# Output projections ahead of SSM steps for the free PSUM bank, and a re-set of the planner's rules

## The chip, the cores and the metric

The kernel runs on one core of a Trainium2 chip. The metric is the device time in microseconds; the time before is the median of three runs, 708.05 us (708.03 to 708.15). One more execution was taken with the hardware profiler; the numbers of the profile come from it.

The core has five engines that run side by side and meet at semaphores: TensorE (PE; its weight loads are shown apart as PEld), VectorE (DVE), ScalarE (ACT), GpSimd (POOL) and SyncE (SP), which here issues DMAs.

## The reference

Two independent branches share one launch, and their outputs stand side by side in a [1, 2048, 1280] bf16 result.

- **Branch A, a diagonal state-space model (SSM).** x is [2048, 640]. Per state, `Lam_bar = exp(dt * Lam)` with complex `Lam`; the input matrix is scaled by `(Lam_bar - 1) / Lam`; the recurrence is `h[t] = Lam_bar * h[t-1] + B_bar x[t]`, and `y[t] = 2 Re(C h[t]) + D * x[t]`.
- **Branch B, attention with 32 query heads of width 20 and one shared key and value head.** `q = x wq`, `k = x wk`, `v = x wv`; `softmax(q k^T / sqrt(20)) v` for every head without a mask; then the heads, 640 wide, times `wo`.

## The kernel before

**Order.** The kernel is written out by a planner that runs on the host while the program is built. `Schedule` simulates the engines with a duration for each step (`Op`); whenever an engine is free, `pick` chooses among the ready steps the one with the lowest `prio`. On TensorE a step in another tiling mode gets 1.2 added to a priority above 1, and a step that would run more than `slack["pe"]` ns into a due urgent step is held back. `Emitter` then writes each engine's stream in that order, with semaphores where data demand them. So the constants of the planner set only the order, and which engine takes a tile; the work itself is fixed. `planned` made 32 plans, each with due times jittered by up to `SPREAD` tiles, replayed each with random DMA delays, and kept the best by its own estimate.

**Attention.** The scores are 2048 tiles of 128 keys x 512 query columns (4 query blocks x 8 groups of 4 heads x 16 key chunks x 4 heads). `attention` goes through them in steps. A step uses one of two sets of three PSUM banks (`CHUNKS = (3, 3)`, tiles `SC`): TensorE writes up to three score tiles as matmuls on 32 rows of the array each (`score`, mode S). ScalarE then takes the exponential of two or three of them at once into `PR` (`fill`, line 1489). VectorE can take the third bank instead ("own" tile): it makes a bf16 pattern from the score with an integer add and max into a buffer of `BIG` (`fill_d`, line 863), and three shifted copies of it, most of them made two at a time by GpSimd as 64-bit integer adds (`copy`, line 1804) and the rest by VectorE. The four copies are multiplied with four scaled versions of V (`VS`), so a VectorE tile needs four V matmuls and a ScalarE tile one (`VP`). V matmuls run four at once on 32 columns each (`pv`, mode C) into the bank `MB` kept for them.

**Which tiles go to VectorE.** `want_own` and `want_d` allow one if the count stays under `SHARE` = 0.29 of (tiles so far - 16), not in the last 20 tiles, if copy buffers are free and if `behind()` is false; `in_time` asks that VectorE can read the third bank at most `SPARE` ns after ScalarE ends with the other two; `WAITING` bounds the third-bank tiles not yet read. `behind()` is true when the next SSM unit's last step has not started `LAG` tiles after its due tile and an SSM step marked late could be run.

**The other work.** Everything else takes turns on one free PSUM bank (`MISC = 1`), handed out by `manager`: of the tasks whose due tile has come and which are ready, the one with the lowest class, and among these the one due first. Class 1 are query projections (`q_task`); class 2 are the SSM tasks: ten products `C B` (`cb_task`), 20 units of five state blocks in four time blocks (`unit_task`, followed on VectorE by rotations, two scans and `W`), and 20 output steps (`y_task`). The output projections `o_task` of the query blocks, five each, were class 2 as well. A task's product steps run as groups of four matmuls, or ride one piece at a time on a score step's free rows (`ride`, `board`), as long as more than `KEEP_C` steps are left. Copies from PSUM go to `stg` and from there to the output. The last query block's output projections, and three partial sums of them made ahead, end the kernel. Filler matmuls on zeros (`VZ`) keep TensorE active where it would fall idle.

**Queues.** SP issues nearly all DMAs in the planned order; GpSimd's stream has only the library load, constants and the copies.

Of the kernel before, what the change touches and what calls it, by code (L numbers as in the profile page):

```python
# [24 lines left out]
class Op:  # L25
# [5 lines left out]
    def __init__(self, eng, fns, dur, deps=(), prio=5, reads=(), writes=(), prev=None, gate=None, hook=None,  # L31
                 dma_key=None, land=0.0, tail=0.0, mode="F", load=0.0, port=False):
        self.eng, self.fns, self.dur = eng, list(fns), dur
        self.deps, self.prio, self.prev = list(deps), prio, prev
        self.reads, self.writes = list(reads), list(writes)
        self.gate, self.hook = gate, hook
        self.dma_key, self.land, self.tail = dma_key, land, tail
        self.mode, self.load, self.late = mode, load, False
        self.port, self.after, self.due, self.table, self.twice, self.fence, self.lands = port, [], None, None, None, None, None
        self.psum = any(k[0] == "B" and k[1:].isdigit() for k in self.reads)  # L40
        self.start = self.end = None
        self.clear = 1e18
        self.seq = self.idx = 0


class Schedule:
# [13 lines left out]
    EARLIER = {"dve": 40.0, "act": 8.0}  # L60
# [4 lines left out]
    def __init__(self, seed=0):  # L65
        self.rng = random.Random(seed) if seed else None
        self.t = 0.0
        self.pending = {e: [] for e in self.ENGINES}
        self.free = {e: 0.0 for e in self.ENGINES}
        self.order = []  # L70
        self.events = []
        self.procs = []
        self.dma_free = {}
        self.n = 0
        self.mode = None
        self.late_from = 0.0
        self.loads = []
        self.sources = {e: [] for e in self.ENGINES}
        self.slack = {"pe": 60.0, "dve": 150.0}
        self.port_free = {"dve": 0.0, "pool": 0.0}  # L80
        self.port_last = {"dve": None, "pool": None}
        self.port_wanted = False
        self.pipe, self.table = 0.0, None
# [374 lines left out]
NQB, NKC, NGG = 4, 16, 8  # L458
NTILE = NQB * NGG * NKC * 4
# [6 lines left out]
class Build:  # L466
# [73 lines left out]
        shares.update({f"OPT{k}": [f"BA{i}_{c}" for i in range(2) for c in range(NC)] for k in self.EARLY_O})  # L540
        return shares

    SPREAD = 12.0
    PLANS, REPLAYS = 32, 12

    def planned(self):

        best = None
        gc.disable()
        for seed in range(self.PLANS):  # L550
            plan = copy.copy(self)
            plan.s = Schedule(seed)
            plan.program()
            try:
                plan.s.run()
            except RuntimeError:
                continue
            cold = self.COLD * self.quiet(plan.s.order)
            if best is not None and max(op.end for op in plan.s.order) + cold > best[0] + self.MARGIN:
                continue  # L560
            em = Emitter(self.nc, plan.s.order, [b.key for b in plan.banks], self.shared())
            em.plan()
            end = sum(em.replay(random.Random(k)) for k in range(self.REPLAYS)) / self.REPLAYS + cold
            if best is None or end < best[0]:
                best = (end, em)
        gc.enable()
        return best[1]
# [160 lines left out]
    def quads(self):  # L728
        return self.QUADS and self.started

    GRAIN, KEEP_C = 256, 5

    def ride(self, bank, steps):

# [697 lines left out]
    def fill_now(self, op, i, n):  # L1432
# [6 lines left out]
        if s.t >= op.due or not self.can_d() or len(self.d_free()) < len(self.SHIFTS):  # L1439
            return True  # L1440
        if len(self.d_banks()) >= self.WANT:
            return True
# [5 lines left out]
                    return False  # L1448
        return True

    WANT = 1

    def fill(self, op, i):
        p = self
        t, banks = self.slots[i]
        n = min(self.cap[i], NTILE - self.tile_n)
        extra, used, own = [], set(), None
        if n == 3 and self.want_own() and self.in_time(i):
            own = self.take_d(used)
        if own is not None:  # L1460
            n = 2
        while len(extra) < 4 - self.cap[i] and self.want_d(len(extra), own is not None):
            m = self.take_d(used)
            if m is None:
                break
            extra.append(m)
        tiles = [self.take_tile(used) for _ in range(n)]
        h = self.pr_take(n)
        keys = [f"PR{h.index + x}" for x in range(n)]
        ents = []  # L1470
        for x, m in enumerate(tiles):
            b, kc, j = self.score(op, m, t[:, 512 * x:512 * x + 512], banks[x])
            ents.append((b, kc, j, p.PR[:, h.index + x, :]))
        first = [] if own is None else [self.fill_d(op, own, banks[2])]
        if first:
            other = self.slot_last[1 - i][0]
            begin = self.s.t + self.mmt(512, 4) + 200
            if other.eng == "act":
                begin = max(begin, other.start + other.dur if other.start is not None else self.s.t + other.dur)
            first[0].due = begin + 2 * (0.8333 * 1024 + 64) - self.REFILL  # L1480
        for m in extra:
            self.fill_d(op, m)
        n_mm = len(op.fns)
        self.board(op, used)
        op.reads = sorted(set(op.reads))
        op.dur = self.mmt(512, n_mm + (len(op.fns) > n_mm))
        op.load = 128.0 * n_mm
        dst = p.PR[:, h.index:h.index + n, :]
        ex = self.act(lambda e: e.activation(dst, t[:, 0:512 * n], ACT.Exp, scale=1.0 / UNIT),  # L1489
                      0.8333 * 512 * n + 64, table="exp",  # L1490
                      deps=[op], reads=[b.key for b in banks[:n]], writes=keys, prio=0.5,
                      gate=lambda: all(x.taken and x.left == 0 and self.s.done(x.users) for x in h.prev))

        def on_start(_):
            h.taken, h.left, h.prev = True, n, []
            self.waiting.remove(h)
        self.waiting.append(h)
        ex.hook = on_start
        self.slot_last[i] = [ex] + first
        for (b, kc, j, rhs), key in zip(ents, keys):  # L1500
            self.pvq[b][j].append((p.VP[:, kc, 0:32], kc, rhs, key, ex, h, "VP"))
            self.pv_filled[b] += 1
# [29 lines left out]
        return any(x is not None and x.taken and x.left for x in self.owner[at:at + 3]) \  # L1532
            or any(x.left for h in self.waiting for x in h.prev)

    WAITING = 2
    REFILL = 900.0

    def want_own(self):
        if self.tile_n >= NTILE - self.LAST or self.d_count + 1 > self.SHARE * (self.tile_n - 16) or self.behind():
            return False  # L1540
        if sum(1 for o in self.firsts if o.start is None) >= self.WAITING:
            return False
# [3 lines left out]
    def in_time(self, i):  # L1546
# [7 lines left out]
        for o in self.firsts:  # L1554
            if o.start is None:
                at = max(at, s.seen(o.deps[0], "dve")) + 605
        return at + 605 + 110 <= begin + 2 * 512 * 0.8333 + 64 + self.SPARE

    SPARE = 100
    firsts = []  # L1560
    LAG = 120

    def behind(self):

        while self.next_unit < NQB * NC:
            w = self.w_op.get(divmod(self.next_unit, NC))
            if w is None or w.start is None:
                return self.tile_n > self.unit_due[divmod(self.next_unit, NC)] + self.LAG \
                    and any(o.late and self.s.ready(o) is not None for o in self.s.pending["dve"])
            self.next_unit += 1  # L1570
        return False

# [32 lines left out]
        self.tile_n += 1  # L1605
        return 64 * b + 4 * self.rem[b][j].popleft() + j

    EARLIER, LATER = 4, 5
    AHEAD, CAP, ROOM = 10, 2, 4

    def d_block(self):

# [52 lines left out]
            op.reads = sorted(set(op.reads))  # L1665
        return Op("pe", [], self.mmt(512), prio=self.ALONE, mode="S", load=128.0, hook=hook)

    ALONE, TASK, PV = 1.9, 0.95, 2.0
    EV, P1, COPY, COPY1 = 0.52, 0.5, 0.56, 0.6
    P1OWN = 0.42  # L1670
    CLOSE, PVEV = 0.3, 0.3

# [87 lines left out]

    BACKLOG = 9
    LAST = 20
    POOL_LAST = 10

    def pool_source(self):

        s = self.s
        can = [d for d in self.d_open if d[1].end is not None and s.seen(d[1], "pool") <= s.t]
        if not can or len(self.d_free()) < 2 or self.tile_n > NTILE - self.POOL_LAST or self.adds_op.start is None:
            return None  # L1770
# [499 lines left out]
        self.cb_done = True  # L2270

    C_DUE = 200
    CB_FROM, CB_STEP = 300, 20

    def cb_of(self, cd, lo, hi):
        return self.xbT[:, cd, lo:hi]
# [146 lines left out]
        return lambda: all(o.start is not None for o in ops)  # L2423


    Q_FROM, Q_STEP = (0, 30, 110, 190), 15
    SSM_FROM, SSM_TO, Y_STEP, GRACE = 150, 1780, 20, 40
    unit_due = {}

    def background(self):  # L2430
        T = self.tasks
# [9 lines left out]
                T.append((64 * (b + 1), 0, lambda b=b: self.den_ready(b), lambda bank, b=b: self.den_task(b, bank)))  # L2441
        for qb in range(NQB):
            for k in range(5):
                T.append((512 * (qb + 1) + 30 + 40 * k if qb < NQB - 1 else NTILE - 8, 2, lambda qb=qb: self.o_ready(qb),
                          lambda bank, qb=qb, k=k: self.o_task(qb, (4, 0, 1, 2, 3)[k], bank)))
        for k in self.EARLY_O:
            T.append((NTILE - 72, 2, lambda: self.parts_ready(), lambda bank, k=k: self.o_task(NQB - 1, k, bank, True)))
# [8 lines left out]
        for i, (unit, tb, c, ri) in enumerate(jobs):  # L2456
# [5 lines left out]
            n = i - len(jobs) + NC  # L2462
# [4 lines left out]
        if rng is not None:  # L2467
            T[:] = [(t[0] + (rng.uniform(-self.SPREAD, self.SPREAD) if 0 < t[0] < self.SSM_TO else 0.0),) + t[1:] for t in T]
        T.sort(key=lambda t: t[0])
# [115 lines left out]
```

## Time and profile before

| | |
|---|---|
| Median of 3 runs | 708.05 us |
| Profiled execution, first to last instruction | 707.2 us |
| ScalarE / TensorE busy | 691.6 us / 692.6 us |
| VectorE / GpSimd busy | 618.2 us / 466.5 us |
| Score tiles by ScalarE / VectorE | 1479 / 569 |
| First and last exponential start | 18.7 us, 698.2 us |

Busy time counts overlapping instructions once. Consecutive exponentials overlap in the profile, and the ends of matmuls are modelled, so neither share says by itself that an engine can do no more: the distance from one start to the next does. A row of a group gives engine, operation, output and inputs, shape, count, then busy us, mean ns of one, and the idle time of that engine just before, with what ended it. A row of a stage gives the stretch in us, its length, and for each engine the busy time with the number of instructions.

### The profile page before, as it was taken

Reading aid. Unit: us, or ns where it says so; the run is one execution under the profiler, and the core shown is the slowest. Engines: PE = TensorE matmul, PEld = TensorE weight load, DVE = VectorE, ACT = ScalarE, POOL = GpSimd, SP = SyncE. Lnnn points to the kernel's source line nnn. Section 1 sums busy time; section 2 is a strip of 40 time slices with the busy share of each in tenths; the row PEclk is TensorE's granted clock in tenths of the full one; section 3 lists DMA queues with packets and bytes.
Section 4 is the critical chain, followed back from the end, with each engine's and each line's share of the span. In section 5 each row is a group of like instructions: output and inputs, shape, how many; then the busy total and the mean of one; then the engine's idle time right before and its main releaser. Section 6 shows DMA issues by size and latency. Waiting matters only on the chain.

```text
span 707.2 us, 26749 instructions
## 1 busy us (share of the span) xinstructions
PE 692.6 (98%) x11246; PEld 248.8 (35%) x11248; DVE 618.2 (87%) x1181; ACT 691.6 (98%) x705; POOL 466.5 (66%) x794
## 2 busy tenths in 40 slices
PE   9999999999999999999999999999999999999997
PEld 5322233443233433333433332324333333343323
DVE  7899899999988878868779998999999999977794
ACT  7999999999999999999999999999999999999996
POOL 4266682037877667745967777787777768678881
PEclk9999999999999999999999999999999999999999
DMA  9677551020120001101401010120000001110001
GB/s 224 160 162 174 124 136 53 27 45 9 32 66 12 9 19 28 52 8 34 62 20 29 18 27 25 44 56 18 16 14 20 13 23 27 39 27 19 24 15 39
DMA packets 77589, 34.44 MB, mean 49 GB/s; under 512 B 58350, under 2 KB 77470, under 8 KB 77470
## 3 DMA queue, kind: packets, MB, share of 16 engines
q1 hardware_dynamic: 76506, 32.44, 19.2%
q8 instruction: 90, 1.47, 0.9%
q10 hardware_dynamic: 964, 0.29, 0.2%
q14 instruction: 29, 0.24, 0.1%
HBM read 11.53 MB, written 9.75 MB: 30 GB/s over the span
## 4 chain that ended last, share of the span: by engine, by line
ACT 56%; PE 42%; issue 0%; DVE 0%
ACT PR L1489 56%; PE MB L726 17%; PE MB L796 10%; PE SC L726 10%; PE MB L806 4%; PE SC L1154 1%; PE SC L722 0%; PE MB L1271 0%; DVE mab L1160 0%; DVE BIG L863 0%; PE SC L1210 0%; ACT PR L2051 0%; DVE pvsb L858 0%; DVE M L862 0%; DVE PR L964 0%
## 5 line engine op out<-in xcount | busy, mean ns | idle before, releaser
L1489 ACT ACTIVATE PR<-SC 128x1024 bf16<-128x1024 f32 (+1 forms) x681 | 676.7, 1199 | 5.0 <-PE SC L726 4.2
L1804 POOL INT64_ADD BIG<-BIG x759 | 454.2, 615 | 214.8 <-DVE BIG L863 75.0
L863 DVE TENSOR_SCALAR BIG<-SC 128x512 int16<-128x512 f32 x534 | 360.7, 686 | 61.2 <-PE SC L726 53.1
L726 PE MATMUL SC<-QT,KT 32*128 32x512 bf16 x2013 | 266.4, 384 | 6.6 <-ACT PR L1489 3.3
L726 PE MATMUL MB<-BIG,VS 128*32 128x512 bf16 x2276 | 254.6, 384 | 0.4 <-DVE pvsb L1871 0.3
L726 PE MATMUL MB<-PR,VP 128*32 128x512 bf16 x1479 | 205.0, 385 | 0.0
L726 PEld LDWEIGHTS SC<-QT,KT 32*128 32x128 bf16 x2013 | 68.0, 90 | 179.2 <-ACT PR L1489 117.5
L726 PEld LDWEIGHTS MB<-BIG,VS 128*32 128x32 bf16 x2276 | 59.3, 94 | 63.5 <-issue 42.1
L726 PEld LDWEIGHTS MB<-PR,VP 128*32 128x32 bf16 x1479 | 48.9, 94 | 49.7 <-issue 38.5
L796 PE MATMUL MB<-CT,W 128*32 128x320 bf16 (+2 forms) x1000 | 53.6, 301 | 0.1
L863 DVE TENSOR_SCALAR BIG<-BIG 128x1024 int16<-128x1024 int16 (+1 forms) x100 | 39.8, 424 | 2.6 <-PE MB L726 2.3
L796 PE MATMUL MB<-CA,W 128*32 128x512 bf16 (+1 forms) x640 | 36.4, 302 | 0.6 <-issue 0.5
L796 PE MATMUL MB<-xaT,BA 128*32 128x256 bf16 x800 | 31.8, 275 | 0.2 <-DVE BIG L1311 0.2
L806 PE MATMUL MB<-xaT,BT 32*128 32x256 bf16 x160 | 30.9, 272 | 0.7 <-ACT PR L1489 0.7
L806 PE MATMUL MB<-diagD,xaT 32*128 32x128 bf16 x320 | 31.3, 217 | 0.0
L796 PEld LDWEIGHTS MB<-CT,W 128*32 128x32 bf16 x1000 | 23.0, 96 | 15.0 <-issue 6.8
L806 PEld LDWEIGHTS MB<-diagD,xaT 32*128 32x128 bf16 x320 | 17.7, 92 | 29.4 <-ACT PR L1489 20.4
L796 PE MATMUL MB<-xaT,BT 128*32 128x256 bf16 x640 | 26.7, 274 | 0.0
L2056 DVE CAST stg<-MB 128x512 bf16<-128x512 f32 x35 | 23.9, 683 | 1.8 <-PE MB L796 1.4
L858 DVE TENSOR_TENSOR prod<-MB,tab 128x1024 bf16<-128x1024 f32 x20 | 24.3, 1217 | 0.9 <-PE SC L726 0.6
L863 DVE TENSOR_SCALAR BIG<-MB 128x512 int16<-128x512 f32 x35 | 23.8, 680 | 0.1
L796 PE MATMUL MB<-WO,OP 128*32 128x128 bf16 (+1 forms) x480 | 23.4, 301 | 0.0
(169 smaller groups left out, 473.8 us busy)
## 6 DMA issues: line engine op xcount, KB each, us to landing
out_dram<-stg SPq DMA_DIRECT2D x31, 128.0 KB, 1.8
qd<-BIG SPq DMA_DIRECT2D x20, 128.0 KB, 2.2
QT<-qd SPq DMA_DIRECT2D x28, 80.0 KB
OP<-pvsb SPq DMA_DIRECT2D x105, 20.0 KB
rdP<-recs SPq DMA_DIRECT2D x105, 20.0 KB
lbd<-BA SPq DMA_DIRECT2D x5, 320.0 KB, 3.0
CT<-in_B_x_dram SPq DMA_DIRECT2D x2, 640.0 KB, 5.3
BA<-in_A_B_re_dram SPq DMA_DIRECT2D x1, 800.0 KB, 7.9
```

Source lines behind the costliest of these rows:

```text
L726: return lambda e: e.matmul(out, lhsT=lhsT, rhs=rhs, start=start, stop=stop, **kw)
L796: x = e.matmul(out[32 * j:32 * j + 32], lhsT=lhsT[:, 32 * j:32 * j + 32], rhs=rhs, start=start, stop=r.end is tag, tile_position=(0, 32 * ...
L806: return lambda e: e.matmul(out, lhsT=lhsT[at], rhs=rhs[at], start=False, stop=r.end is tag, tile_position=(32 * row, 0), skip_group_check ...
L858: return lambda e: e.tensor_tensor(out, a, b, op)
L863: return lambda e: e.tensor_scalar(out, a, s1, s2, op0=op0, op1=op1)
L1154: prev = self.pe([lambda e, x=x, c=c, n=n, at=at: e.matmul(bank.cols(n * x, n * x + n), lhsT=p.wks[:, 128 * c:128 * c + 128], rhs=p.xbT[:, ...
L1489: ex = self.act(lambda e: e.activation(dst, t[:, 0:512 * n], ACT.Exp, scale=1.0 / UNIT), 0.8333 * 512 * n + 64, table="exp", deps=[op], re ...
L1804: op.fns.append(lambda e: e.int64_add(words(dst), words(src), add))
L2056: ev = self.dve(lambda e: e.tensor_copy(st, bank.ap), 645, deps=[prev], reads=[bank.key], writes=[key], prio=self.EV, gate=(lambda: last.e ...
```

## The change

The order's rules are set anew; no step is added or removed.

- Output projections of the first three query blocks go from class 2 to class 1, due at 512 (qb + 1) + 31.4 + 40 k.
- `behind()`: `LAG` 120 to 190.4 tiles, and a late SSM step counts only if it can start within `SOON` = 2731 ns.
- Admission of VectorE tiles: `WAITING` 2 to 3, `SPARE` 100 to 148, `REFILL`, `AHEAD`, `LATER`. The cap `SHARE` stays. `MISC_FIRST` is new and off.
- TensorE's `slack` 60 to 192.8 ns; `KEEP_C` 5 to 3; priorities `ALONE`, `PV`, `COPY1`; `POOL_LAST` 10 to 6; due times `CB_FROM`, `CB_STEP`, `Q_STEP`, `Y_STEP`, `GRACE`.
- One plan, with seed 69701 and a jitter of 14.5 tiles, in place of the best of 32 with 12.

```diff
-        self.slack = {"pe": 60.0, "dve": 150.0}
+        self.slack = {"pe": 192.807, "dve": 150.0}
...
-    SPREAD = 12.0
-    PLANS, REPLAYS = 32, 12
+    SPREAD = 14.468
+    SEEDS, REPLAYS = (69701,), 12
...
-        for seed in range(self.PLANS):
+        for seed in self.SEEDS:
...
-    GRAIN, KEEP_C = 256, 5
+    GRAIN, KEEP_C = 256, 3
...
-        if n == 3 and self.want_own() and self.in_time(i):
+        if n == 3 and not (self.MISC_FIRST and self.want_d() and self.can_d()) and self.want_own() and self.in_time(i):
...
-    WAITING = 2
-    REFILL = 900.0
+    WAITING = 3
+    REFILL = 905.623
...
-    SPARE = 100
+    SPARE = 148.045
     firsts = []
-    LAG = 120
+    LAG, SOON = 190.385, 2730.774
...
-                    and any(o.late and self.s.ready(o) is not None for o in self.s.pending["dve"])
+                    and any(o.late and (self.s.ready(o) or 1e18) <= self.s.t + self.SOON for o in self.s.pending["dve"])
...
-    EARLIER, LATER = 4, 5
-    AHEAD, CAP, ROOM = 10, 2, 4
+    EARLIER, LATER = 4, 6
+    AHEAD, CAP, ROOM = 14, 2, 4
...
-    ALONE, TASK, PV = 1.9, 0.95, 2.0
-    EV, P1, COPY, COPY1 = 0.52, 0.5, 0.56, 0.6
+    ALONE, TASK, PV = 1.686, 0.95, 1.9
+    EV, P1, COPY, COPY1 = 0.52, 0.5, 0.56, 0.83
...
-    POOL_LAST = 10
+    POOL_LAST = 6
...
-    CB_FROM, CB_STEP = 300, 20
+    CB_FROM, CB_STEP = 358.689, 15.665
...
-    Q_FROM, Q_STEP = (0, 30, 110, 190), 15
-    SSM_FROM, SSM_TO, Y_STEP, GRACE = 150, 1780, 20, 40
+    Q_FROM, Q_STEP = (0, 30, 110, 190), 12.835
+    O_FROM, O_STEP, O_CLASS = 31.404, 40, 1
+    SSM_FROM, SSM_TO, Y_STEP, GRACE = 150, 1780, 16.662, 48.136
...
-                T.append((512 * (qb + 1) + 30 + 40 * k if qb < NQB - 1 else NTILE - 8, 2, lambda qb=qb: self.o_ready(qb),
+                T.append((512 * (qb + 1) + self.O_FROM + self.O_STEP * k if qb < NQB - 1 else NTILE - 8, self.O_CLASS if qb < NQB - 1 else 2, lambda qb=qb: self.o_ready(qb),
```

More of the change, by code (lines that the diff above doesn't have):

```diff
@@ L1449, in fill_now @@
         return True
-    WANT = 1
+    WANT, MISC_FIRST = 1, False
     def fill(self, op, i):
```

## The prediction

> **What bounds the kernel now.** I read the page first, for the shares and for the chain that ended last.
>
> ```profile
> span 707.2 us, 26749 instructions
> PE 692.6 (98%) x11246; PEld 248.8 (35%) x11248; DVE 618.2 (87%) x1181; ACT 691.6 (98%) x705; POOL 466.5 (66%) x794
> ACT 56%; PE 42%; issue 0%; DVE 0%
> ```
>
> Two engines look full, so the second view is the groups of instructions with the shapes kept apart. It says how the 2048 score tiles are shared.
>
> ```profile
> L1489 ACT ACTIVATE PR<-SC 128x1024 bf16<-128x1024 f32 x562 | 528.2, 1115 | 4.4 <-PE SC L726 4.2
> L1489 ACT ACTIVATE PR<-SC 128x1536 bf16<-128x1536 f32 x118 | 168.8, 1603 | 0.6 <-PE MB L726 0.5
> L863 DVE TENSOR_SCALAR BIG<-SC 128x512 int16<-128x512 f32 x534 | 360.7, 686 | 61.2 <-PE SC L726 53.1
> L863 DVE TENSOR_SCALAR BIG<-MB 128x512 int16<-128x512 f32 x35 | 23.8, 680 | 0.1
> L726 PE MATMUL MB<-BIG,VS 128*32 128x512 bf16 x2276 | 254.6, 384 | 0.4 <-DVE pvsb L1871 0.3
> L726 PE MATMUL MB<-PR,VP 128*32 128x512 bf16 x1479 | 205.0, 385 | 0.0
> ```
>
> VectorE turned 534 + 35 = 569 tiles into probabilities (2276 = 4 x 569 confirms it: such a tile is multiplied with V four times), ScalarE 1479, in exponentials two or three tiles wide. Third comes what one exponential costs from start to start, since they overlap and the mean of one is longer than its turn. Two stretches hold one width only (windows 112 to 130.1 and 156 to 163.4), and the view of the exponential's line has the first and last start.
>
> ```profile
> L1489 ACT ACTIVATE PR<-SC 128x1536 bf16<-128x1536 f32 x15 | 20.5, 1742 | 0.0
> L1489 ACT ACTIVATE PR<-SC 128x1024 bf16<-128x1024 f32 x9 | 8.4, 1131 | 0.0
> L1489 ACT ACTIVATE PR<-SC x681: 787/1127/1830, 18.7 to 698.2; 128x1024 bf16<-128x1024 f32 x142, 128x1536 bf16<-128x1536 f32 x28, 128x512 bf16<-128x512 f32 x1
> ```
>
> A turn is (20.5 - 1.74) / 14 = 1.340 us for three tiles and (8.4 - 1.13) / 8 = 0.909 us for two, so a tile taken off ScalarE is worth 0.431 us. From the first start to the last are 679.5 us, of which 562 x 0.909 + 118 x 1.340 = 669.0 are turns and about 10.5 us are gaps. Head 18.7 us, stream 679.5, tail 9.0: that is the span. The median of the runs, 708.05, is 0.85 us above it. So the time is the number of ScalarE tiles, plus gaps, plus head and tail. The chain of waits says who sets the pace.
>
> ```profile
> ACT PR L1489 <- PE SC L726: 4.2, 6, 1.4
> PEld SC L726 <- ACT PR L1489: 117.5, 286, 0.7
> PEld SC L726 <- DVE BIG L863: 36.6, 86, 0.6
> PEld MB L726 <- issue: 84.3, 371, 0.4
> ```
>
> The score matmuls were released by ScalarE 286 times, the exponentials by TensorE visibly 6 times. ScalarE leads; TensorE follows closely.
>
> **The change part by part.** No work is removed. The planner keeps its cap of 0.29 x (tiles so far - 16) VectorE tiles and stops them 20 tiles before the end, so at most 0.29 x 2012 = 583 are allowed; 569 were taken. Where the rest was lost is in the busy time of VectorE on the score banks by stage (columns: stretch, its length, busy time and, in brackets, instructions, nearly all of them such tiles; then granted clock, DMA share, GB/s):
>
> ```profile
> 20.00:110.00 90.00, 43.28 (x66) 1.00 0.61 142
> 110.00:160.00 50.00, 7.07 (x12) 1.00 0.15 38
> 160.00:210.00 50.00, 29.98 (x44) 1.00 0.14 32
> 210.00:410.00 200.00, 106.39 (x157) 1.00 0.13 27
> 410.00:610.00 200.00, 127.92 (x191) 1.00 0.11 27
> 610.00:700.00 90.00, 51.73 (x77) 1.00 0.08 20
> ```
>
> *Withholding (behind: LAG 120 to 190, SOON).* Between 110 and 160 us 12 tiles were taken where the next 50 us took 44. There the rule withholds them: the first SSM unit is due at tile 150, so from tile 270 on: at three tiles and 679.5 / 680 = 1.0 us a step that is 18.7 + 90 = 109 us. With LAG 190 it is tile 340, some 70 / 3 = 23 steps of 0.9 to 1.3 us later, so past 130 us, when the first unit's W stood written already (128.4 us in a row below). SOON then drops operations not ready within 2.7 us. Of the 30 lost tiles, between 15 and 30 come back there. Later stages caught up at 48 a 50 us; the cap allows no more than 583, so the net gain lies between 0 (another rule binds) and +14. I take +11, near the upper end: the 191-tile stage shows that the engines can run above the cap's rate. 11 x 0.431 = 4.7 us less.
>
> What the returned tiles cost stands in the engines' busy time of those two stages, the filler matmuls in the first one, and a piece of the timeline with V matmuls in groups of four (the first two rows have PE, PEld, DVE, ACT and POOL in this order, the third PE, PEld and DVE):
>
> ```profile
> 110.00:160.00 50.00, 47.72 (x820) 18.98 (x821) 46.84 (x99) 50.00 (x42) 9.81 (x16) 1.00 0.15 38
> 160.00:210.00 50.00, 48.98 (x775) 16.66 (x767) 45.94 (x83) 50.00 (x53) 39.12 (x66) 1.00 0.14 32
> 110.00:160.00 50.00, 4.34 (x100) 2.29 (x100) 0.00 (x0) 1.00 0.15 38
> 302.38 1.05 PE L726 MATMUL MB<-BIG,VS 128*32 128x512 bf16 x16
> L1804 POOL INT64_ADD BIG<-BIG x759 | 454.2, 615 | 214.8 <-DVE BIG L863 75.0
> ```
>
> Four groups of four take 1.05 us, so (1.05 - 0.38) / 3 = 0.22 us a group; a VectorE tile needs three quarter groups more, 0.17 us. Thirty of them put 5.0 us on TensorE between 110 and 160 us, where it idled 2.3 us and ran 4.3 us of fillers that exist to keep it awake: hidden. Later stages then hold some 19 tiles fewer, 3.2 us less there. Copies go to GpSimd (0.615 us a pair; busy 9.8 of 50 us in that stage): hidden. VectorE itself idled 3.2 us there and gets 30 x 0.686 = 20.6: up to 17.4 us of SSM preparation move later. What waits for it is the first rival.
>
> *Admission of a third-bank tile (WAITING 2 to 3, SPARE 100 to 148, REFILL, AHEAD, LATER).* More may be taken; each may free its bank 0.048 us later. The refill of a bank set has about one exponential, 0.909 less a matmul's 0.38 us, of room: nothing on the path. This helps to reach the cap; bounds 0 and the 0.431 us a tile counted above.
>
> *KEEP_C 5 to 3.* More product steps ride on score steps' free rows. Each ridden step saves a 0.22 us group on TensorE; with one rider a step at most 681 / 4 = 170 steps, so between 0 and 37 us of TensorE time. On ScalarE's pace: 0 taken, as TensorE is not ahead of it; it widens the cover.
>
> *TensorE slack 60 to 193 ns.* A V step may run into a due score step by 0.13 us more. Covered by the same 0.5 us of room; if not, each uncovered case is a gap of 0.13 us, and it also fills TensorE's idle. Taken as 0, bounds -5.3 (half the gaps) and +5.3.
>
> *Ranks.* ALONE 1.686 and PV 1.9 keep their order with the 1.2 added for a change of mode (1.686 < 1.9 + 1.2 and 1.9 < 1.686 + 1.2, as with 1.9 and 2.0); COPY1 0.83 passes no rank in use after the start; MISC_FIRST is off. All 0.
>
> *Output projections (O_CLASS 2 to 1).* Fifteen steps take the one free bank ahead of SSM steps. Their work is the same; they only swap with it.
>
> ```profile
> L796 PE MATMUL MB<-WO,OP 128*32 128x512 bf16 x240 | 18.5, 382 | 0.0
> L796 PE MATMUL MB<-WO,OP 128*32 128x128 bf16 x240 | 4.9, 221 | 0.0
> L858 DVE TENSOR_TENSOR W<-prod x20: 413/418/678, 128.4 to 613.6; 128x512 bf16<-128x512 bf16 x20
> L2283 DVE CAST BIG<-MB x10: 473/482/492, 156.7 to 227.5; 128x320 bf16<-128x320 f32 x10
> L2056 DVE CAST stg<-MB x35: 667/682/693, 248.0 to 672.2; 128x512 bf16<-128x512 f32 x35
> ```
>
> One turn is (18.5 + 4.9) / 15 = 1.6 us of matmuls and a 0.68 us copy, 2.2 us: five put the SSM steps back 11 us. The last output copy, 672.2, lies 26.0 us before the last exponential: 0, up to that margin. Their stores and the scatters that wait for freed buffers move earlier on SP, past SSM stores at most; the last stages have little DMA: 0. CB_FROM 358.7 to 499.7 lies ahead of when those steps ran (copies 156.7 to 227.5 us, behind C's scaling): 0. Q_STEP, O_FROM, Y_STEP, GRACE move due times by under 17 tiles: 0.
>
> *POOL_LAST 10 to 6.* One GpSimd pair, 0.6 us, more or less in the tail: 0, bounds +-0.6. *One seed with a spread of 14.5 in place of the best of 32 plans.* Another order of the same kinds of steps. What order alone can do is bounded by the gaps: -10.5 if all went, about +10.5 if they doubled; 0 taken.
>
> Sum: 708.05 - 4.7 = 703.3 us.
>
> **The rivals.**
>
> *SSM work slips past the stream (slower).* The 17.4 us of delayed preparation and 11 us of output projections make 28.4, over the margin of 26.0 us; from 26.0 on a last SSM output step stands behind the last exponential. Its sixteen groups are 3.5 us, the copy 0.7, the store 1.8, and the three partial sums kept for the last block slide too.
>
> ```profile
> out_dram<-stg SPq DMA_DIRECT2D x31, 128.0 KB, 1.8
> L2020 DVE COPY BA<-MB 128x512 f32<-128x512 f32 x3 | 2.1, 688 | 2.4 <-PE MB L722 2.4
> ```
>
> 703.3 + 6.0 + 2.1 = 711.4 us. Against it: LAG still withholds tiles when the chain is over 190 tiles late, and later stages hold fewer VectorE tiles than before.
>
> *TensorE becomes the bound (slower).* It is at 98%, and changes between score and V steps cost it 84.3 / 371 = 0.227 us of idle loads each. If all 11 tiles came as lone score steps, 22 changes are 5.0 us, and their V work 1.8: 6.8, less the 4.3 us of fillers, with ScalarE's gain lost in gaps: 710.5 us. For it: the wait row of 371. Against it: 286 releases by ScalarE. The Trainium skill, "TensorEngine Tiling (Array Packing)", section "Tiling Modes", says that a change of tiling mode drains TensorE; the trace agrees (0.227 us), and by that rule alone the price of this rival is the 5.0 us just worked out. Against this rival speaks the skill's "Perfetto Trace Analysis", section "Identifying the Most-Contended Engine": matmul busy time is a poor measure, loads' busy share a good one; by its 35% TensorE would have room, 1.8 us more would vanish, and the time would be 703.3. The drains count in neither share, so I leave this rival a chance.
>
> *No tile is gained.* The total is held by other rules (free copy buffers, admission in time; 157 tiles in 200 us with VectorE not full speak for it), and only the order changes: 708.0 us.
>
> *The gaps shrink too.* All 14 tiles come (-6.0) and riding and slack take half of the gaps (-5.3): 696.8 us.
>
> **How the numbers follow.** Forecast (700 to 705.5 us): 0.57. Gaps shrink too: 0.11. No tile gained: 0.08. SSM slip: 0.13. TensorE bound: 0.11. The prediction is the likeliest, 703.3. Range 699.5 to 710.5: it takes in the forecast, no gain and TensorE bound, and leaves out most of the gap case and the slip. A measurement here can tell about 0.2%, 1.4 us; so faster 0.68, within 0.08, slower 0.24.
>
> **What would show it.** Right: the count of two exponential widths falls to some 1468 tiles on ScalarE, V matmuls on VectorE tiles rise to about 2320; 110 to 160 us holds 27 to 42 VectorE tiles and fewer than 50 fillers; last output copy before about 690 us; head and tail within 1 us. Wrong: 2276 unchanged; output copies after 698 us; exponentials waiting on score matmuls for well over 4.2 us.

## The result, and the profile after

The changed kernel takes 702.93 us (median of 4 runs, 702.72 to 704.23) against 708.1 us before: a ratio of 0.9924, with a 95% interval of 0.991 to 0.9938, so the gain is clear of the noise. The prediction was 703.3 us.

The profile of the changed kernel has much the same busy shares; of its chain that ended last, TensorE now has a larger share than ScalarE.

```profile
span 702.4 us, 27010 instructions
PE 687.0 (98%) x11350; PEld 248.4 (35%) x11350; DVE 620.6 (88%) x1180; ACT 685.9 (98%) x700; POOL 484.2 (69%) x822
PE 55%; ACT 39%; DVE 2%; SPq 1%; DMA 1%; issue 0%; DVEq 0%
```

The groups with the shapes kept apart, and the line of the exponential with its count and its first and last start:

```profile
L1489 ACT ACTIVATE PR<-SC 128x1024 bf16<-128x1024 f32 x560 | 526.7, 1109 | 5.1 <-PE SC L726 4.4 <-PE MB L726 0.3
L1489 ACT ACTIVATE PR<-SC 128x1536 bf16<-128x1536 f32 x116 | 166.9, 1549 | 0.7 <-PE MB L726 0.5 <-PE SC L726 0.2
L863 DVE TENSOR_SCALAR BIG<-SC 128x512 int16<-128x512 f32 x542 | 365.8, 685 | 56.8 <-PE SC L726 49.0
L863 DVE TENSOR_SCALAR BIG<-MB 128x512 int16<-128x512 f32 x38 | 25.7, 677 | 0.1
L726 PE MATMUL MB<-BIG,VS 128*32 128x512 bf16 x2320 | 253.5, 383 | 0.6 <-DVE pvsb L1871 0.3
L726 PE MATMUL MB<-PR,VP 128*32 128x512 bf16 x1468 | 206.3, 384 | 0.0
L1489 ACT ACTIVATE PR<-SC x676: 1017/1118/1703, 20.1 to 691.8; 128x1024 bf16<-128x1024 f32 x137, 128x1536 bf16<-128x1536 f32 x32
```

VectorE has 542 + 38 = 580 tiles (2320 / 4), 11 more, and ScalarE 1468. With the turns of 0.909 and 1.340 us from the prediction, the 675 exponentials ahead of the last (three tiles wide) are 560 x 0.909 + 115 x 1.340 = 663.1 us, where before had 669.0. The stream from 20.1 to 691.8 is 671.7 us, so the gaps are 8.6 us, before 10.5. In this execution the head is 1.4 us longer (20.1 against 18.7) and what follows the last start 1.6 us longer (10.6 against 9.0), in part because the last exponential is three tiles wide and was one tile wide before. Together: -5.9 - 1.9 + 1.4 + 1.6 = -4.8, the difference of the spans.

The tiles came in other places than I had said. VectorE on the score banks by stage (stretch, length, busy time and count, granted clock, DMA share, GB/s):

```profile
20.00:110.00 90.00, 39.16 (x60) 0.99 0.60 140
110.00:160.00 50.00, 15.31 (x23) 1.00 0.13 36
160.00:210.00 50.00, 27.81 (x42) 1.00 0.14 34
210.00:410.00 200.00, 117.34 (x174) 1.00 0.13 30
410.00:610.00 200.00, 123.72 (x185) 1.00 0.11 27
610.00:700.00 90.00, 49.18 (x75) 1.00 0.08 21
```

From 110 to 160 us there are 11 more, not 15 to 30; 17 more came from 210 to 410 us, and the other four stages have 6, 2, 6 and 2 fewer. The filler matmuls in the stage 110 to 160 us (PE and PEld busy) grew from 100 to 140, and the first `W` of the SSM work was written later, its last one no later:

```profile
110.00:160.00 50.00, 5.90 (x140) 3.18 (x140) 0.00 (x0) 1.00 0.13 36
L858 DVE TENSOR_TENSOR W<-prod x20: 415/418/668, 150.9 to 612.7; 128x512 bf16<-128x512 bf16 x20
L2056 DVE CAST stg<-MB x35: 674/681/692, 232.9 to 664.3; 128x512 bf16<-128x512 f32 x35
```

The first W moved from 128.4 to 150.9 us, the last from 613.6 only to 612.7, and the last output copy from 672.2 to 664.3. The waits still have ScalarE ahead: it released the score matmuls 215 times (286 before), while the exponentials waited for them visibly 5 times.

```profile
PEld SC L726 <- ACT PR L1489: 90.0, 215, 0.8
PEld MB L806 <- ACT PR L1489: 66.9, 187, 0.7
PEld MB L726 <- issue: 77.5, 339, 0.4
ACT PR L1489 <- PE SC L726: 4.7, 5, 3.5
```

### The profile page after: what moved, and what is told of

Same layout as the page of the kernel before. It is cut to its first block, busy times and chain, and to the rows that moved or that the text cites. A ratio compares the mean times of both kernels' runs of the same rounds, so it can differ in the third digit from the quotient of the medians.

```text
span 702.4 us, 27010 instructions
## 1 busy us (share of the span) xinstructions
PE 687.0 (98%) x11350; PEld 248.4 (35%) x11350; DVE 620.6 (88%) x1180; ACT 685.9 (98%) x700; POOL 484.2 (69%) x822
## 4 chain that ended last, share of the span: by engine, by line
PE 55%; ACT 39%; DVE 2%; SPq 1%; DMA 1%; issue 0%; DVEq 0%
ACT PR L1489 39%; PE MB L726 21%; PE MB L796 15%; PE SC L726 10%; PE MB L806 7%; SPq L711 1%; DVE BIG L863 1%; DMA wvr<-in_B_wv_dram 1%; PE MB L722 1%; DMA qd<-BIG 1%; PE SC L722 0%; PE SC L796 0%; SPq L707 0%; DVE PR L858 0%; PE SC L1210 0%
## 5 line engine op out<-in xcount | busy, mean ns | idle before, releaser
L1804 POOL INT64_ADD BIG<-BIG x787 | 471.9, 615 | 191.2 <-DVE BIG L863 49.7
L863 DVE TENSOR_SCALAR BIG<-SC 128x512 int16<-128x512 f32 x542 | 365.8, 685 | 56.8 <-PE SC L726 49.0
L726 PE MATMUL SC<-QT,KT 32*128 32x512 bf16 x2010 | 264.3, 385 | 6.7 <-ACT PR L1489 3.7
L726 PE MATMUL MB<-BIG,VS 128*32 128x512 bf16 x2320 | 253.5, 383 | 0.6 <-DVE pvsb L1871 0.3
L726 PE MATMUL MB<-PR,VP 128*32 128x512 bf16 x1468 | 206.3, 384 | 0.0
L726 PEld LDWEIGHTS SC<-QT,KT 32*128 32x128 bf16 x2010 | 66.8, 91 | 153.1 <-ACT PR L1489 90.0
L726 PEld LDWEIGHTS MB<-BIG,VS 128*32 128x32 bf16 x2320 | 61.6, 95 | 63.3 <-issue 38.9
L726 PEld LDWEIGHTS MB<-PR,VP 128*32 128x32 bf16 x1468 | 49.5, 94 | 45.6 <-issue 32.5
L863 DVE TENSOR_SCALAR BIG<-BIG 128x1024 int16<-128x1024 int16 (+1 forms) x88 | 35.3, 419 | 1.5 <-POOL BIG L1804 0.8
L806 PE MATMUL MB<-xaT,BT 32*128 32x256 bf16 x184 | 35.6, 273 | 0.2 <-ACT PR L1489 0.2
L806 PE MATMUL MB<-diagD,xaT 32*128 32x128 bf16 x320 | 31.4, 217 | 0.2 <-ACT PR L1489 0.2
L796 PEld LDWEIGHTS MB<-CT,W 128*32 128x32 bf16 x1000 | 22.6, 96 | 14.5 <-issue 5.9
L863 DVE TENSOR_SCALAR BIG<-MB 128x512 int16<-128x512 f32 x38 | 25.7, 677 | 0.1
L796 PE MATMUL MB<-WO,OP 128*32 128x512 bf16 (+1 forms) x456 | 23.1, 304 | 0.0
```

The lines of the kernel that those rows point to most:

```text
L726: return lambda e: e.matmul(out, lhsT=lhsT, rhs=rhs, start=start, stop=stop, **kw)
L796: x = e.matmul(out[32 * j:32 * j + 32], lhsT=lhsT[:, 32 * j:32 * j + 32], rhs=rhs, start=start, stop=r.end is tag, tile_position=(0, 32 * ...
L806: return lambda e: e.matmul(out, lhsT=lhsT[at], rhs=rhs[at], start=False, stop=r.end is tag, tile_position=(32 * row, 0), skip_group_check ...
L863: return lambda e: e.tensor_scalar(out, a, s1, s2, op0=op0, op1=op1)
L1804: op.fns.append(lambda e: e.int64_add(words(dst), words(src), add))
```

## The experiments

My theory: time follows the number of tiles that VectorE takes, 0.431 us each. Rivals: the seed, the gaps, TensorE's own pace, and SSM work pushed to the end. A variant of the changed kernel "with 32 seeds" picks its order as the kernel before does, so that no variant gains from a searched seed. The tile counts below are V matmuls on VectorE tiles divided by four, from the profiles. "Tile theory" is the expectation from the count. Each ratio is against runs of the kernel before taken beside that variant (medians 707.9 to 708.6 us), so losses between variants are differences of ratios, times 708 us, unless both were taken on the same occasion.

| run | edit | VectorE tiles | us | ratio to before |
|---|---|---|---|---|
| before | | 569 | 708.1 | |
| after | all rules, seed 69701 | 580 | 702.93 | 0.9924 |
| e5_rules32 | all rules, 32 seeds | 580 | 702.46 | 0.9925 |
| e1_slack60 | without the slack | 564 | 711.35 | 1.005 |
| e2_keep5 | without KEEP_C | 568 | 708.78 | 1.0007 |
| e3_lag120 | without LAG, SOON | 573 | 706.73 | 0.9972 |
| e4_oclass2 | without O_CLASS | 577 | 705.28 | 0.9955 |
| e16_admit | without admission | 571 | 706.07 | 0.9975 |
| e8_share28 | all, lower cap | 562 | 708.8 | 1.0012 |
| e9_lag_off | all, no withholding | 580 | 712.76 | 1.0068 |
| e6_slack_alone | before + slack | 571 | 706.85 | 0.9974 |
| e7_lag_alone | before + LAG, SOON | 569 | 708.8 | 1.0011 |
| e10_lag_slack_keep | before + three rules | 575 | 704.85 | 0.9967 |
| b1 | a version made from these | 582 | 701.88 | 0.9915 |

**The seed.**

```diff
-    SEEDS, REPLAYS = (69701,), 12
+    SEEDS, REPLAYS = range(32), 12
```

> The changed rules with the order picked as before, best of 32 seeds by the planner's own estimate, in place of seed 69701. The order it picks gives VectorE 580 tiles, as many as the changed kernel. Tile theory (each tile moved from ScalarE to VectorE is worth 0.431 us, the rest is worth nothing): 702.9 us, within 1. Rival, the seed carries the gain: 704.5 to 708.

702.46 us (701.94 to 703.0), ratio 0.9925 (0.991 to 0.994). The rules carry the gain; a best of 32 does as well as the seed named. The variants below are compared with e5. It has 560 and 116 exponentials of two and three tiles, the last one three wide, as the changed kernel has:

```profile
L1489 ACT ACTIVATE PR<-SC x676: 1017/1120/1703, 18.2 to 690.3; 128x1024 bf16<-128x1024 f32 x144, 128x1536 bf16<-128x1536 f32 x25
```

So its turns are 663.1 us, its stream 672.1, its gaps 9.0 and its tail 700.2 - 690.3 = 9.9 us.

**One part taken out: the slack.**

```diff
-        self.slack = {"pe": 192.807, "dve": 150.0}
+        self.slack = {"pe": 60.0, "dve": 150.0}
```

> The changed rules, best of 32 seeds, with TensorE's slack back at 60 ns. The order gives VectorE 564 tiles, 16 fewer. My prediction put the slack at 0 on ScalarE's pace: 702.9. Tile theory: 702.9 + 16 x 0.431 = 709.8. If the slack also closed gaps in ScalarE's stream, still more than 709.8, up to 713, with the exponentials' wait for score matmuls over 4.7 us.

711.35 us, ratio 1.005 (1.0033 to 1.0066): slower than the kernel before, and 8.9 us over e5, of which 16 tiles are 6.9. My zero for this edit is refuted. The exponentials and V matmuls of e1, and one of its waits:

```profile
L1489 ACT ACTIVATE PR<-SC 128x1024 bf16<-128x1024 f32 x553 | 520.9, 1114 | 3.5 <-PE SC L726 2.2 <-PE MB L726 0.7 <-PE MB L806 0.2
L1489 ACT ACTIVATE PR<-SC 128x1536 bf16<-128x1536 f32 x126 | 179.8, 1567 | 1.4 <-PE MB L726 1.3
L726 PE MATMUL MB<-BIG,VS 128*32 128x512 bf16 x2256 | 248.6, 384 | 0.3 <-DVE pvsb L1871 0.2
L1489 ACT ACTIVATE PR<-SC x679: 1018/1137/1778, 18.6 to 699.6; 128x1024 bf16<-128x1024 f32 x137, 128x1536 bf16<-128x1536 f32 x33
ACT PR L1489 <- PE MB L726: 2.0, 4, 0.9
```

Turns ahead of the last are 553 x 0.909 + 125 x 1.340 = 670.2 us, the stream 681.0, the gaps 10.8, which is 1.8 more than e5's: about the 2 us beyond the count. The visible waits of the exponentials for score matmuls are 2.2 us, not over 4.7, so that part of the expectation was wrong. They waited as much for V matmuls (the row L726 on `MB`; these read the buffers `PR` that an exponential writes): 2.0 us in four waits, where the waits of e5 list none.

**The cap alone.**

```diff
-    SHARE = 0.29
+    SHARE = 0.28
```

> The changed rules, best of 32 seeds, with only the cap lowered, SHARE 0.29 to 0.28: VectorE gets 562 tiles, 18 fewer, and all other rules stay. Tile theory: 702.9 + 18 x 0.431 = 710.7. Rival, TensorE sets the pace: 18 x 0.17 = 3.0 us less V work on TensorE, so 700 to 703. In between (705 to 708) if a tile off ScalarE is partly paid back in gaps.

708.8 us, ratio 1.0012 (1.0003 to 1.0022), 6.3 over e5, for 18 tiles: 0.35 us a tile, or 0.25 to 0.44 by the ends of the two intervals. The rival that TensorE sets the pace is out: with 18 tiles fewer, TensorE had less V work and the kernel got slower. So had VectorE (603.3 us busy, in e5 621.5). In e8:

```profile
L1489 ACT ACTIVATE PR<-SC 128x1024 bf16<-128x1024 f32 x539 | 512.9, 1111 | 2.6 <-PE SC L726 2.1
L1489 ACT ACTIVATE PR<-SC 128x1536 bf16<-128x1536 f32 x136 | 198.5, 1558 | 0.2 <-PE SC L726 0.2
L726 PE MATMUL MB<-BIG,VS 128*32 128x512 bf16 x2248 | 253.6, 383 | 0.9 <-DVE pvsb L1871 0.7 <-POOL BIG L1804 0.2
L1489 ACT ACTIVATE PR<-SC x675: 1018/1130/1717, 19.1 to 698.1; 128x1024 bf16<-128x1024 f32 x137, 128x1536 bf16<-128x1536 f32 x32
L726 PE MATMUL MB<-KT,VZ x348: 272/273/389, 25.3 to 698.1; 128*32 128x256 bf16 x172, 128*32 128x512 bf16 x2
```

Here the last exponential is two tiles wide, so the turns ahead of it are 538 x 0.909 + 136 x 1.340 = 671.3, the stream 679.0, the gaps 7.7. The fillers rose to 348 from e5's 240: where TensorE was spared V work, more zeros ran. Gaps 1.3 us smaller than e5's 9.0 make up for most of the 1.5 us that are missing of the 7.8. Against e1, with nearly the same count (562 and 564), the gaps are 3.1 us smaller and the time 2.5 us: that is about the slack's own share, as far as two orders can be compared that differ in more than the slack.

**Withholding taken away.**

```diff
-    LAG, SOON = 190.385, 2730.774
+    LAG, SOON = 100000, 2730.774
```

> The changed rules, best of 32 seeds, with withholding by lateness taken away (LAG so large that it never holds). VectorE gets 580 tiles as in the changed kernel, but some 45 of them between 110 and 160 us. Tile theory: 702.9 us. Rival, SSM work slips to the end: last output copy after 690 us, gaps or a longer tail, 708 to 713 us.

712.76 us, ratio 1.0068 (1.0053 to 1.0084), with 580 tiles: the slip of the first rival, at full size. A wait of e9, its last output copies, and the start of its W:

```profile
L2056 DVE CAST stg<-MB x35: 619/682/693, 232.3 to 706.5; 128x512 bf16<-128x512 f32 x35
L858 DVE TENSOR_TENSOR W<-prod x20: 415/464/660, 216.2 to 656.1; 128x512 bf16<-128x512 bf16 x20
ACT PR L2051 <- PE SC L722: 8.3, 2, 7.6
110.00:160.00 50.00, 23.25 (x35) 1.00 0.11 31
L1489 ACT ACTIVATE PR<-SC x674: 778/1102/1670, 18.7 to 698.2; 128x1024 bf16<-128x1024 f32 x140, 128x1536 bf16<-128x1536 f32 x29
```

From 110 to 160 us it took 35 tiles, not the 45 expected here, but within the 27 to 42 that I had expected of the change. The first W then came at 216.2 us, the last output copy 8.3 us after the last exponential started, and from that start to the end are 712.0 - 698.2 = 13.8 us instead of e5's 9.9. The rest of the loss is mostly gaps in the stream: 679.5 us less 552 x 0.909 + 121 x 1.340 = 663.9 of turns leaves 15.6, where e5 had 9.0. So withholding is worth its price; the relaxed form still keeps the SSM chain in time (last output copy at 664.3 us in the changed kernel).

**The other parts taken out.**

```diff
-    GRAIN, KEEP_C = 256, 3
+    GRAIN, KEEP_C = 256, 5
```

> The changed rules, best of 32 seeds, with KEEP_C back at 5 (fewer steps ride on score steps). VectorE gets 568 tiles, 12 fewer. My prediction put KEEP_C at 0: 702.9. Tile theory: 702.9 + 12 x 0.431 = 708.1. If riding helps only by closing gaps: over 708.1.

708.78 us, ratio 1.0007 (0.9996 to 1.0017): 0.8% lost, 5.8 us; 12 tiles are 5.2.

```diff
-    LAG, SOON = 190.385, 2730.774
+    LAG = 120
...
-                    and any(o.late and (self.s.ready(o) or 1e18) <= self.s.t + self.SOON for o in self.s.pending["dve"])
+                    and any(o.late and self.s.ready(o) is not None for o in self.s.pending["dve"])
```

> The changed rules, best of 32 seeds, with the old withholding (LAG 120, no SOON). VectorE gets 573 tiles, 7 fewer. My prediction gave this part the whole gain: back to 707 to 708. Tile theory: 702.9 + 7 x 0.431 = 705.9. Fewer tiles between 110 and 160 us than the 23 of the changed kernel.

706.73 us, ratio 0.9972 (0.9962 to 0.9982): 0.47% lost, 3.3 us; 7 tiles are 3.0. From 110 to 160 us it took 14 tiles, fewer than 23 as expected, and its first W came at 135.3 us.

```diff
-    O_FROM, O_STEP, O_CLASS = 31.404, 40, 1
+    O_FROM, O_STEP, O_CLASS = 31.404, 40, 2
```

> The changed rules, best of 32 seeds, with output projections back in the SSM steps' class. VectorE gets 577 tiles, 3 fewer. My prediction: 0, so 702.9; tile theory 704.2. Rival, the projections ahead are what helps: 706 or more.

705.28 us, ratio 0.9955 (0.994 to 0.997): 2.1 us lost; 3 tiles are 1.3, and the rival's 706 was not reached. The intervals of e4 and e5 touch, so the output projections' turn is worth 0 to 4 us.

```diff
-    WAITING = 3
-    REFILL = 905.623
+    WAITING = 2
+    REFILL = 900.0
...
-    SPARE = 148.045
+    SPARE = 100
...
-    EARLIER, LATER = 4, 6
-    AHEAD, CAP, ROOM = 14, 2, 4
+    EARLIER, LATER = 4, 5
+    AHEAD, CAP, ROOM = 10, 2, 4
```

> The changed rules, best of 32 seeds, with the admission of third-bank tiles as before (WAITING 2, SPARE 100, REFILL 900, AHEAD 10, LATER 5). VectorE gets 571 tiles, 9 fewer. Tile theory: 702.5 + 9 x 0.431 = 706.3. If admission matters by more than the count: over 707.5.

706.07 us, ratio 0.9975 (0.9965 to 0.9985): 3.5 us lost; 9 tiles are 3.9. The case of over 707.5 us did not come.

**One part alone, and three.** The kernel before with the slack of 192.807 only:

> The kernel before with one rule changed: TensorE's slack 60 to 192.8 ns; best of 32 seeds as before. VectorE gets 571 tiles, 2 more than before. Tile theory: 708.05 - 0.9 = 707.2. If the slack closes gaps in ScalarE's stream by itself: 703 to 706, with fewer fillers than before's 172 matmuls.

706.85 us, ratio 0.9974 (0.9964 to 0.9983): 1.8 us won; 2 tiles are 0.9, and the rest may again be the slack's own, though 706.85 lies outside the 703 to 706 us expected if it were so. The fillers went up, not down, from 172 to 288, so that part of the expectation was wrong. The kernel before with the new withholding only:

> The kernel before with only the withholding rule changed (LAG 190, SOON); best of 32 seeds. My prediction gave this rule the whole gain, so 703.3. But the order picked gives VectorE 569 tiles, as many as before (more between 110 and 160 us, fewer from 160 to 210): tile theory 708.0, no change.

708.8 us, ratio 1.0011 (1.0002 to 1.002): no gain. The stages 110 to 160 and 160 to 210 us of e7 on the score banks, and its W:

```profile
110.00:160.00 50.00, 13.48 (x20) 1.00 0.10 26
160.00:210.00 50.00, 21.43 (x32) 1.00 0.16 37
L858 DVE TENSOR_TENSOR W<-prod x20: 408/418/671, 149.3 to 605.4; 128x512 bf16<-128x512 bf16 x20
```

The 8 tiles won in the first stage are lost as 12 in the next. The first W came at 149.3 us, 21 us later than before, and I take it that the units then late withheld the tiles again; but the changed kernel's first W came as late (150.9 us), and it took 42 tiles in that stage. So a late W alone does not explain the loss, and which of the other rules prevents it stays open. The withholding, the slack and KEEP_C together on the kernel before:

> The kernel before with three rules changed together: withholding (LAG 190, SOON), TensorE's slack 192.8, KEEP_C 3; best of 32 seeds. VectorE gets 575 tiles, 6 more than before. Tile theory: 708.0 - 2.6 = 705.4. If slack and riding also close gaps, 703 to 705.

704.85 us, ratio 0.9967 (0.9953 to 0.9981), as the count says.

**Edits without effect.** Put back one at a time in the changed kernel, ALONE and PV, and COPY1, give the same instructions in the same order on every engine; CB_FROM and Q_STEP put back as well change nothing more, and POOL_LAST only instructions near the end. None was run, so the value of POOL_LAST is not shown. Y_STEP and GRACE were put back in no run.

**A version made from this.** More slack, less spare, a longer LAG, two riding steps open at once, and a searched seed:

```diff
-        self.slack = {"pe": 192.807, "dve": 150.0}
+        self.slack = {"pe": 232.457, "dve": 150.0}
...
-    LAG, SOON = 190.385, 2730.774
+    LAG, SOON = 213.86, 2730.774
...
-    SPARE = 148.045
+    SPARE = 126.65
...
-    BACKLOG = 9
+    BACKLOG = 8
...
-    OPEN = 1
+    OPEN = 2
...
-    SEEDS, REPLAYS = (69701,), 12
+    SEEDS, REPLAYS = (3344,), 12
```

(REFILL, SPREAD, Q_STEP, SSM_FROM and Y_STEP moved a little too.)

> A version made from what the runs showed: the changed rules with slack 232, SPARE 127, LAG 214, BACKLOG 8, OPEN 2, SSM_FROM 130 and seed 3344. VectorE gets 582 tiles, 2 more than the changed kernel. Tile theory: 702.5 - 0.9 = 701.6; if its gaps are smaller too, 700.5.

701.88 us (700.38 to 705.06), ratio 0.9915 (0.9898 to 0.9932). It is faster than the kernel before by 0.85%; from the changed kernel (0.991 to 0.9938) it can't be told apart.

## Why the prediction was right, and where its steps were not

- **The price of a tile: right; the count: right, but by luck.** 11 tiles were taken as +11 and came as 580 - 569 = 11. That the number is exact is luck: the step that gave it, the next one, was wrong about where the tiles come from. The price held: the tiles moved 5.9 us of turns by the trace, with 1.6 us given back behind the last exponential's start, against 4.7. The one run that moved the count by itself, e8, gives 0.35 us a tile (0.25 to 0.44), with 0.431 near the upper end. Over the runs that take one part out, the losses by the ratios (5.8, 3.3, 2.1, 3.5 us, and 8.9 for the slack) follow the count at 0.431 (5.2, 3.0, 1.3, 3.9, 6.9) within 2.0 us.
- **Where the count comes from: wrong in part.** The step gave the whole gain to withholding, with "between 15 and 30" tiles back from 110 to 160 us. There 11 came back; and alone that rule gave nothing (e7). In company it is worth 7 tiles (e3). The prediction took the first unit's W as written by 128.4 us, when the tiles would come back; but that was W with the tiles withheld. The first W came at 135.3 us with the old rule among the new ones (e3, 14 tiles in that stage), at 147.8 to 152.1 us with the new rule (20 to 28 tiles, in e7, the changed kernel and its variants), and at 216.2 us without any (35 tiles): the longer VectorE is let take tiles, the later the SSM work. That a late W then withholds the next tiles is argued; e7 lost 12 of them in the next stage, the changed kernel with a W as late only 2.
- **Slack "taken as 0" and KEEP_C "0 taken": wrong.** They were priced for what they cost ScalarE's path, and not for what they do to the count: 16 and 12 tiles in company, and the slack 1.8 to 3.1 us of gaps besides (e1 against e5 and against e8). Admission, taken as help, is worth 9. The parts don't add: 16 + 12 + 7 + 3 + 9 = 47 tiles, for 11 in all, so most of them pay only beside the others.
- **The cover by fillers: wrong in sign.** I expected fewer than 50 fillers from 110 to 160 us, as V work would take their place; there were 140. That TensorE had room there was right. The V work of 11 tiles is only 1.9 us, and the other matmuls of the stage became fewer: 761 in all with the 140 fillers, so 621, where before had 820 - 100 = 720. That they are fewer because SSM steps came later (the first W 22.5 us later) is argued, not tested.
- **Output projections at 0: nearly right**; 0 to 4 us.
- **Ranks, CB_FROM, Q_STEP, the seed: right.** POOL_LAST, Y_STEP and GRACE at 0 were not tested.
- **Gaps at 0: 1.9 us off**, inside the bound. The head and the tail, which were to stay within 1 us, were 1.4 and 1.6 us longer in the profiled execution; in e5, with the same rules, they were 18.2 and 9.9 us and within 1 us of before.
- **The rivals.** SSM slip: real, but only when withholding is gone (e9, 712.8 us where 711.4 was worked out). TensorE as the bound: refuted by e8, though the chain that ended last now names it for 55%. No tile gained: that is what e7 shows for withholding alone. The Trainium skill's "Perfetto Trace Analysis", section "Identifying the Most-Contended Engine", distrusts matmul busy time, and e8 agrees with it: TensorE at 98% in e5 was no bound.

That the 32-seed variants compare orders each picked for itself leaves some scatter: the largest gap between count and time is, apart from e9, 2.0 us (e1), and no run separates it further.

## What to carry to other kernels

Where two engines share one kind of tile, price a tile by the start-to-start distance on the engine that leads, and count tiles; here that explained every variant but the one without withholding to within 2 us. A rule that withholds work protects a chain that every piece of withheld work, once let through, delays: here relaxing it alone gave nothing, relaxing it beside the other rules gave 7 tiles, and taking it away cost more than the whole change gave. Rules that seem to cost nothing on the leading engine can still decide how many tiles another engine is let take.

## What the runs showed that I had not expected

The profiled execution of the changed kernel is the longest of its four; the other three spanned 700.8 to 701.1 us, this one 702.4. They have no profile, but the head of this one stands out: its first exponential started 1.4 us later than before's. The chain that ended last has a wait for one load there, and the stage from 15 to 20 us a granted clock of 0.84 (columns as for the stages in the prediction).

```profile
11.66 4.68 DMA wvr<-in_B_wv_dram
15.00:20.00 5.00, 3.80 (x58) 1.58 (x57) 3.11 (x11) 1.60 (x3) 1.05 (x2) 0.84 1.03 357
```

The kernel before had 1.00 there:

```profile
15.00:20.00 5.00, 4.72 (x79) 2.49 (x78) 4.16 (x17) 3.54 (x7) 1.57 (x3) 1.00 1.05 363
```

The wait for the load left TensorE idle for 1.2 us, up to 16.4 us; the clock fell some 2 us later, while TensorE was busy, and was 0.50 from 19 to 21 us. The Trainium skill's "TensorE: Matmul & The Clock Gate", "Part 1: The HAM clock gate", says that the array runs at half rate after an idle window of about 3.4 us. The trace shows the half rate, but no idle time of that length in the head. Nor does the load explain the clock: e6 has the same wait, 4.56 us in its chain and 1.1 us of idle TensorE, and kept a clock of 1.00; its first exponential started at 19.4 us. e5, with the changed rules in another order, has no such wait, and started at 18.2. So what took the clock down in this execution stays open, and no run separates what the load alone cost the head.
